# One transposition for both fp16 halves of x, one load for a pair's q and k, and two larger times in the plan of an attention and MLP kernel

## The chip, the cores and the metric

The kernel runs on one core of one Trainium2 chip. The metric is the device time of one execution in microseconds (us), taken as the median of the runs shown. Of one execution there is a profile: for every engine when each instruction ran and what ended its waits. The engines are PE (matrix products; PEld is its weight loads), DVE and ACT (elementwise and reductions, and activation functions), POOL, and SP, which here issues nearly all the DMAs. SPq is SP's queue of DMA issues.

## The reference

```
def phi(x):
    proj = np.einsum('bhsd,df->bhsf', x, w_phi)
    proj = proj - np.max(np.abs(proj), axis=-1, keepdims=True)
    return np.concatenate([np.exp(proj), np.exp(-proj)], axis=-1)
q_p, k_p = (phi(q), phi(k))                          # (8, 8, 576, 256)
kv = np.einsum('bhsf,bhsd->bhfd', k_p, v)
z = np.sum(k_p, axis=2)
num = np.einsum('bhsf,bhfd->bhsd', q_p, kv)
den = np.einsum('bhsf,bhf->bhs', q_p, z)[..., None] + 1e-06
x = num / den, heads side by side: (4608, 512)
h = x @ w_in                                         # w_in (512, 2048)
sp = np.maximum(h, 0.0) + np.log1p(np.exp(-np.abs(h)))
out = (h * erf(sp)) @ w_out                          # w_out (2048, 512)
```

All inputs and the output are float32. The batch is 8, with 8 heads of 64 and 576 tokens.

## The kernel before, in words

Two streams share PE. The attention stream works on pairs of heads, p = 0 to 31, four pairs to a batch, in three groups g of 384 tokens. The MLP stream works on blocks of 256 tokens, in steps n of half a block's hidden width. A large matrix product in float32 is replaced by three in fp16: each operand is split in a high half and a low half, and high by high, high by low and low by high are summed.

For a pair and a group, `k_piece` projects q and k (PE, line L438), takes the row maxima (DVE, tile m, L409) and subtracts them (DVE, tiles uk and uq, L415); ACT writes exp of uk into kp (L359). `t_piece` turns uq, so that features lie on partitions. For the first eight pairs PE does it; from pair 8 on `turn` does: DVE splits the float32 words into 16-bit halves (tile pl, L483), a DMA transposition on SP's queue turns them (plt<-pl, L485, six blocks of 128 columns), and DVE puts them together again (ut<-plt, L486). ACT writes exp of ut into qp (L359). `kv_piece` multiplies kp and v (PE, L352), and `n_piece` multiplies qp and kv (PE, L352), divides by the denominators (DVE, tiles dn and xf) and writes x as two fp16 halves, xth (high) and xtl (low, DVE L561). `x_piece` turns x for the MLP: for each piece of at most 128 tokens one DMA transposition of xth into xh and one of xtl into xl, both on SP's queue (L605), two blocks of 128 columns each.

In the MLP stream `h_chunk` multiplies xh and xl by wih and wil (PE, L342, 128x256), ACT copies the sums out (tile big, L672), softplus and erf follow on DVE and ACT, and `o_chunk` multiplies the gated halves gh and gl by woh and wol (PE, L342, 128x512). The erf gate is one block on ACT: a table load, two activations (L693) and a table load back (L694).

`load_pair` brings a pair's q and k as (two copies of 64 rows beside each other in DRAM, one DMA for k's 64 partitions and one for q's), and v.

The order of all instructions is set by a planner. Every operation states its engine, a cost, and a time `done` after which what it wrote may be used. `Plan.run` plays these through and, whenever an engine is free, takes the ready operation with the lowest priority number; the times at which it starts them give each engine's order of instructions. On the chip each engine then runs its instructions in that order, and waits where an operand isn't there yet. Two numbers matter below. `SLACK`, added to the time from which a PE operation counts as ready, for the operations of MLP steps after n = 2 and the attention pieces laid between them:

```
n.ready = max(n.ready, t + done + (n.slack + 100.0 if n.eng == "PE" else 0.0))
```

And `done=3000` of the transposition in `turn`. Where the plan leaves PE without work for over `HOLE` = 600 ns, it puts in filler products of a constant tile (bank<-hot, L812), two per 216 ns of the hole.

Of the kernel before, what the change touches and what calls it, by code (L numbers as in the profile page):

```python
# [9 lines left out]
F16 = mybir.dt.float16  # L10
# [7 lines left out]
P = 128  # L18
# [5 lines left out]
TB = 256  # L24
# [17 lines left out]
HALVED = 2 * NPAIR  # L42
AHEAD = 8000.0
TURN = 92.0
SLACK = 1200.0
WARM = 10
HOLE = 600.0
PRINT = None
# [23 lines left out]
class Plan:  # L72
# [21 lines left out]
    def buf(self, kind):  # L94
        return Buf(self, kind)
# [161 lines left out]
def favor_attention_moe(ctx: ExitStack, tc: tile.TileContext, qk, vp, wphi, w_in, w_out, out):  # L257
# [10 lines left out]
    def whole(group, n, shape, dt):  # L268
        slots(group, n, shape, dt)
        plan.kind(group, group)  # L270
# [24 lines left out]
    plan.kind("osb", "half", (("osb",), 3))  # L295
    whole("gh", 4, [P, HW], F16)
    whole("gl", 4, [P, HW], F16)
    whole("xh", 8, [P, 2, TB], F16)
    whole("xl", 8, [P, 2, TB], F16)
    slots("ld", 3, [P, 1152], F32)  # L300
    plan.kind("st", "ld", (("st",), 3))
    plan.kind("hl", "ld", (("hl",), 2))
# [12 lines left out]
    whole("kv", 2, [P, 2, 130], F32)  # L315
    whole("dn", 2, [P, 10], F32)
    whole("xf", 2, [P, 256], F32)
    whole("xth", 2, [P, 5, 2 * P], F16)
    whole("xtl", 2, [P, 5, 2 * P], F16)

    op, buf = plan.op, plan.buf
    PE, DVE, ACT, POOL, SP = "PE", "DVE", "ACT", "POOL", "SP"
# [68 lines left out]
    def load_pair(p):  # L391
        t = buf("st")
        for c in [slice(g * 384, (g + 1) * 384) for g in range(3)] if p == 0 else [slice(0, 1152)]:
            for nm, i in (("k", 1), ("q", 0)):
                rows = slice(i * D, (i + 1) * D)
                op(SP, 450 if p == 0 else 600, lambda c=c, i=i, rows=rows: nc.sync.dma_start(t.t[rows, c], qk[p, rows, i, c]),
                   w=[(t, (nm, c.start))], done=2300, land=500 if p == 0 else 1450)
        stg[p] = t, buf("hl") if p >= HALVED else None
        v = buf("v0" if p < NPAIR else "v")
        op(SP, 400, lambda: nc.sync.dma_start(v.t[:, 0:650], vp[p]), w=[v], done=2400, land=1650)  # L400
        vsb[p] = v
# [17 lines left out]
    def project(p, g):  # L419
        kind = "pj" if p >= NPAIR else "p0"  # L420
        src, hl = stg[p]
        both = {nm: buf(kind) for nm in "kq"}
        at = 3 * g * P if p == 0 else 0
        loaded = [(src, ("k", at)), (src, ("q", at))]
        cols = slice(3 * g * P, 3 * (g + 1) * P)
        hv = lambda: hl.t.bitcast(F16).rearrange("p (i t) -> p i t", i=2)
        if hl:
            op(ACT, 430, lambda: nc.scalar.copy(hv()[:, 0, cols], src.t[:, cols]), r=loaded, w=[(hl, (g, 0))], off=-AHEAD)
            op(DVE, 470, lambda: nc.vector.tensor_tensor(hv()[:, 1, cols], src.t[:, cols], hv()[:, 0, cols], op=ALU.subtract),
               r=loaded + [(hl, (g, 0))], w=[(hl, (g, 1))], port=True, off=-AHEAD)  # L430

        def block():
            for t in range(3):
                tok = slice((3 * g + t) * P, (3 * g + t + 1) * P)
                terms = [(hv()[:, 0, tok], w1), (hv()[:, 1, tok], w1), (hv()[:, 0, tok], w2)] if hl else [(src.t[:, tok], wst)]
                for x, w in terms:
                    for nm, rows in (("q", slice(0, D)), ("k", slice(D, P))):
                        nc.tensor.matmul(both[nm].t[:, t * P : (t + 1) * P], x[rows], w.t[rows, :],  # L438
                                         start=w is terms[0][1] and x is terms[0][0], stop=w is terms[-1][1] and x is terms[-1][0])

        if hl:
            op(PE, 520, block, r=[(hl, (g, 0)), (hl, (g, 1)), w1, w2], w=[both["k"], both["q"]], done=780, mode=ROWS)
        else:
            op(PE, 680, block, r=loaded + [wst], w=[both["k"], both["q"]], done=990, mode=ROWS)
        yield 520 if hl else 680
        return front("k", p, both["k"]), front("q", p, both["q"])
# [34 lines left out]
    def turn(u):  # L481
        halves, turned, ut = buf("pl"), buf("plt"), buf("ut")
        op(DVE, 490, lambda: nc.vector.tensor_copy(  # L483
            halves.t, u.t.rearrange("p t f -> p (t f)").bitcast(U16).rearrange("p (n h) -> p h n", h=2)), r=[u], w=[halves], port=True)
        op(SP, 1280, lambda: nc.sync.dma_start_transpose(turned.t, halves.t.rearrange("p h n -> p (h n)")), r=[halves], w=[turned], done=3000)  # L485
        op(DVE, 500, lambda: nc.vector.tensor_copy(  # L486
            ut.t.bitcast(U16).rearrange("p (n h) -> p h n", h=2), turned.t.rearrange("p (h t) k -> p h (t k)", h=2)),
           r=[turned], w=[ut], port=True)
        return ut
# [33 lines left out]
    def n_piece(p, g):  # L523
# [4 lines left out]
        if g == 0:  # L528
            nds[p] = ([buf(kind)], buf("dn"))
            if r == 0:  # L530
                xt[p // 2] = (buf("xth"), buf("xtl"))
        banks, dn = nds[p]
        xth, xtl = xt[p // 2]

        def sums(nb, cnt, h):
            d = lambda: dn.t[:, 6 * h : 6 * h + cnt].unsqueeze(2)
# [5 lines left out]
        def normalise(nb, c0, cnt, d0, key, view):  # L542
            x = buf("xf")
            rows = slice(0, D) if key == "tail" else slice(0, P)
            xv = lambda: x.t[rows, 0 : cnt * D].rearrange("p (t e) -> p t e", t=cnt)
            blk = lambda: nb.t[:, c0 : c0 + 65 * cnt].rearrange("p (t e) -> p t e", e=65)
            d = lambda: dn.t[:, d0 : d0 + cnt].unsqueeze(2)
            if key == "tail":
                for h in range(2):
                    own = slice(h * D, (h + 1) * D)  # L550
                    op(DVE, 140, lambda h=h, own=own: nc.vector.tensor_tensor(
                        xv()[:, h, :], nb.t[own, 0:D], dn.t[own, 0:1].to_broadcast([D, D]), op=ALU.mult),
                       r=[nb, (dn, d0 // 6)], w=[(x, h)])
            else:
                op(DVE, 345, lambda: nc.vector.tensor_tensor(
                    xv(), blk()[:, :, 0:D], d().to_broadcast([P, cnt, D]), op=ALU.mult), r=[nb, (dn, d0 // 6)], w=[x])
            if p < EARLY:
                op(ACT, 310, lambda: nc.scalar.copy(view(xth.t), xv()), r=[x], w=[(xth, (r, key))])
            else:
                op(DVE, 215, lambda: nc.vector.tensor_copy(view(xth.t), xv()), r=[x], w=[(xth, (r, key))], port=True)  # L560
            op(DVE, 345 if cnt == 4 else 205, lambda: nc.vector.tensor_tensor(view(xtl.t), xv(), view(xth.t), op=ALU.subtract),  # L561
               r=[x, (xth, (r, key))], w=[(xtl, (r, key))], port=True)

        def bulk(h):
            return lambda x: x[:, 1:5, r * P + h * D : r * P + (h + 1) * D].rearrange("p t e -> p t e")

        def tail(x):
            return x[0:D, 0, r * P : (r + 1) * P].rearrange("p (t e) -> p t e", t=2)

        for t in range(3):  # L570
            T = 3 * g + t
# [15 lines left out]
                kvs.pop(p)  # L587
                nds.pop(p)

    xh, xl = {}, {}  # L590

    def x_piece(b, half, j):
        n = P if j else 64
        t0 = b * S + ((j - 1) * P if j else 512)
        t = t0
        xth, xtl = xt[2 * b + half]
        while t < t0 + n:
            blk = t // TB
            e = min(t0 + n, (blk + 1) * TB)
            key = blk, half  # L600
            if key not in xh:
                xh[key], xl[key] = buf("xh"), buf("xl")
            for dst, src in ((xh[key], xth), (xl[key], xtl)):
                keys = [(src, (r, k)) for r in range(2) for k in (("tail",) if j == 0 else (0, 1))]
                op(SP, 1280, lambda dst=dst, src=src, t=t, e=e, blk=blk: nc.sync.dma_start_transpose(  # L605
                    dst.t[:, :, t - blk * TB : e - blk * TB], src.t[t - t0 : e - t0, j, :]),
                   r=keys, w=[(dst, t - blk * TB)], done=4300 if b == 0 else 2900)
            t = e
        yield 0

# [43 lines left out]
    def h_chunk(n, c):  # L654
# [5 lines left out]
        for k in range(2):  # L660
            f = half * GF + 2 * c + k
            fs = slice(f * P, (f + 1) * P)
            for cc in range(NCC):
                key = cc, f // 4
                xhb, xlb = xh[blk, cc // 2], xl[blk, cc // 2]
                for w, x, wb in ((wih, xhb, 0), (wih, xlb, 0), (wil, xhb, 1)):
                    mm(109, lambda k=k, cc=cc, fs=fs, w=w, x=x: (ps()[:, k, :], w.t[:, cc, fs], x.t[:, cc % 2, :]),
                       [(w, key), x], [b], cc == 0 and x is xhb and not wb, cc == NCC - 1 and wb == 1)
                    yield 109
        q = c % 2  # L670
        h = hs[n, c // 2]
# [3 lines left out]
            first_evac[n] = o  # L675
        if c == 3 and half:
            for v in range(2):
                xh.pop((blk, v))
                xl.pop((blk, v))

    def softplus(n, v):
        L, h = buf("L"), hs[n, v]
# [146 lines left out]
def _heads_first(x):  # L829
    import numpy as np  # L830

    a = x.reshape(B * NPAIR, 2, S, D)
    return np.concatenate([a[:, 0, 512:], a[:, 1, 512:], a[:, 0, :512], a[:, 1, :512]], axis=1)
# [36 lines left out]
```

## Time and profile before

| | |
|---|---|
| median of 3 runs | 1039.39 us (1038.12 to 1039.76) |
| the profiled execution | 1041.25 us, of which the program's span 1039.5 |
| PE busy | 1012.0 us, 97% of the span, 16732 products |
| DVE, ACT busy | 686.6 us (66%), 710.1 us (68%) |
| mean granted TensorE clock | 0.990 |
| DMA, mean busy share by tenths of the span's fortieths | 8578253437314413233221443334341221000000 |
| transpositions on SP's queue | xh 96, xl 96, plt 72 |
| loads of q and k | 62 of 64x1152, 6 of 64x384 |

A row of the timeline gives start and duration in us, the engine (SPq: a DMA issue), the line, the operation with out<-in, and in brackets how long the engine had sat idle before it and what ended that. Rows of equal neighbours are merged (x6). The answers on waits have total, number of times and the longest, in us. A row of a tile or of a line gives the duration of an instruction in ns as min/median/max. A table of windows gives for each stretch its length and the busy time of each engine in us, then the granted clock of PE and the DMA share.

### The profile page before, as it was taken

The numbers are of one execution on the slowest core, as the hardware profiler recorded it, in microseconds if no ns is written. First come the engines' busy times: TensorE is split into PE (matmuls) and PEld (weight loads), VectorE is DVE, ScalarE is ACT, GpSimd is POOL, SyncE is SP. The second block draws the span as 40 slices with busy tenths as digits, with TensorE's granted clock in tenths as the row PEclk, the third lists the DMA queues.
The fourth block names the chain that finished last, engine by engine and source line by source line (L and its number), as shares of the span: only waits on it lengthen the run. The fifth ranks groups of instructions, "written<-read, shape, count | busy, mean of one in ns | idle before, by whom it ended". The sixth has DMA issues, their size and how long they took to land.

```text
span 1039.5 us, 36968 instructions
## 1 busy us (share of the span) xinstructions
PE 1012.0 (97%) x16732; PEld 790.9 (76%) x16732; DVE 686.6 (66%) x1426; ACT 710.1 (68%) x1126; POOL 0.7 (0%) x6
## 2 busy tenths in 40 slices
PE   9988999998999899999999999999999999999998
PEld 6877876776787777777877777878777777777774
DVE  5989989796658764677644878488756863223332
ACT  6868878776767477766766748676767656566671
POOL 0000000000000000000000000000000000000000
PEclk9999999999999999999999999999999999999999
DMA  8578253437314413233221443334341221000000
GB/s 270 133 166 248 83 187 83 81 63 139 77 41 96 97 43 80 53 77 81 62 51 30 86 88 70 77 64 94 75 85 33 43 60 32 12 22 2 22 12 32
DMA packets 120766, 81.81 MB, mean 79 GB/s; under 512 B 103328, under 2 KB 103840, under 8 KB 120608
## 3 DMA queue, kind: packets, MB, share of 16 engines
q1 hardware_dynamic: 120448, 79.38, 32.0%
q8 instruction: 131, 2.15, 0.9%
q14 instruction: 27, 0.22, 0.1%
q10 hardware_dynamic: 160, 0.07, 0.0%
HBM read 46.37 MB, written 9.44 MB: 54 GB/s over the span
## 4 chain that ended last, share of the span: by engine, by line
PE 72%; DVE 11%; DMA 7%; SPq 5%; ACT 3%; issue 1%; DVEq 0%; ACTq 0%
PE bank L342 58%; PE bank L352 9%; DMA plt<-pl 5%; SPq L605 5%; PE bank L438 4%; DVE m L409 2%; PE bank L812 1%; DVE ut L486 1%; DVE half L380 1%; DVE half L382 1%; DVE uq L415 1%; DMA xh<-xth 1%; DVE wol L386 1%; DVE gl L705 1%; DVE pl L483 1%
## 5 line engine op out<-in xcount | busy, mean ns | idle before, releaser
L342 PE MATMUL bank<-xh,wih 128*64 128x256 f16 x2304 | 321.3, 274 | 2.0 <-DMA xh<-xth 2.0
L342 PE MATMUL bank<-xh,wil 128*64 128x256 f16 x2304 | 321.6, 275 | 0.2 <-DVE wil L386 0.2
L342 PE MATMUL bank<-xl,wih 128*64 128x256 f16 x2304 | 321.8, 275 | 0.0
L342 PEld LDWEIGHTS <-wih 128*64 128x64 f16 x4608 | 257.9, 111 | 31.8 <-DMA xh<-xth 2.1
L342 PE MATMUL bank<-wol,gh 128*64 128x512 f16 x1152 | 221.5, 380 | 0.0
L342 PE MATMUL bank<-woh,gh 128*64 128x512 f16 x1152 | 221.4, 380 | 0.0
L342 PE MATMUL bank<-woh,gl 128*64 128x512 f16 x1152 | 221.3, 379 | 0.0
L342 PEld LDWEIGHTS <-gh 128*64 128x64 f16 x2304 | 128.9, 110 | 81.9 <-issue 0.2
L359 ACT ACTIVATE big<-big 128x1024 f32<-128x1024 f32 x144 | 152.2, 1057 | 41.3 <-DVE big L683 38.7
L672 ACT ACTIVATE big<-bank 128x512 f32<-128x512 f32 x144 | 84.9, 592 | 120.1 <-PE bank L342 119.0
L701 DVE TENSOR_TENSOR big<-big,big 128x1024 f32<-128x1024 f32 x72 | 85.7, 1218 | 83.8 <-ACT big L693 83.8
L342 PEld LDWEIGHTS <-wil 128*64 128x64 f16 x2304 | 132.9, 111 | 3.7 <-DVE wil L386 0.8
L409 DVE TENSOR_REDUCE m<-bank 128x3 f32<-128x384 f32 x192 | 100.0, 549 | 23.2 <-PE bank L438 23.0
L342 PEld LDWEIGHTS <-gl 128*64 128x64 f16 x1152 | 66.2, 110 | 53.7
L359 ACT ACTIVATE qp<-ut 128x384 f32<-128x384 f32 x144 | 69.0, 514 | 55.6 <-DVE ut L486 45.1
L683 DVE TENSOR_SCALAR big<-big 128x1024 f32<-128x1024 f32 x72 | 49.6, 689 | 83.1 <-ACT big L672 82.6
L359 ACT ACTIVATE kp<-uk 128x384 f32<-128x384 f32 x144 | 67.6, 513 | 48.1 <-DVE uk L415 47.8
L705 DVE TENSOR_TENSOR gl<-big,gh 128x1024 f16<-128x1024 f32 x72 | 87.4, 1220 | 15.7 <-ACT gh L704 15.5
L352 PE MATMUL bank<-v,kp 128*64 128x65 f32 (+1 forms) x2016 | 85.0, 231 | 10.1 <-ACT kp L359 9.8
L352 PEld LDWEIGHTS bank<-kv,qp 128*64 128x64 f32 x2304 | 81.6, 139 | 16.8 <-ACT qp L359 9.2
L486 DVE COPY ut<-plt 128x768 uint16<-128x768 uint16 x72 | 43.4, 606 | 75.1 <-DMA plt<-pl 72.1
L352 PE MATMUL bank<-kv,qp 128*64 128x65 f32 x2304 | 85.4, 224 | 7.2 <-ACT qp L359 6.7
(52 smaller groups left out, 1056.1 us busy)
## 6 DMA issues: line engine op xcount, KB each, us to landing
ld<-in_qk_dram SPq DMA_DIRECT2D x62, 288.0 KB, 4.7
out_dram<-half SPq DMA_DIRECT2D x36, 256.0 KB, 2.5
v<-in_vp_dram SPq DMA_DIRECT2D x28, 325.0 KB, 4.2
big<-in_moe_w_in_dram SPq DMA_DIRECT2D x16, 512.0 KB, 9.1
big<-in_moe_w_out_dram SPq DMA_DIRECT2D x16, 512.0 KB, 5.1
xh<-xth SPq DMA_TRANSPOSE x96, 2.5
xl<-xtl SPq DMA_TRANSPOSE x96, 2.4
big<-in_vp_dram SPq DMA_DIRECT2D x4, 325.0 KB, 7.1
```

Of the source, the lines that this page charges most:

```text
L342: nc.tensor.matmul(o[half], a[:, half], b, start=start, stop=stop)
L352: nc.tensor.matmul(o[half], a[:, half], b, start=first and c == 0, stop=last and c == 1)
L359: nc.scalar.activation(out_(), in_(), func, **k)
L380: op(DVE, 600, lambda: nc.vector.scalar_tensor_tensor(f.t.bitcast(I32), word(1), -0x40000000, f.t.bitcast(I32), op0=ALU.bitwise_and, op1=A ...
L409: op(DVE, 470, lambda: nc.vector.tensor_reduce(m.t, ps(), axis=AX.X, op=ALU.max, apply_absolute_value=True), r=[b], w=[m])
L438: nc.tensor.matmul(both[nm].t[:, t * P : (t + 1) * P], x[rows], w.t[rows, :], start=w is terms[0][1] and x is terms[0][0], stop=w is terms ...
L486: op(DVE, 500, lambda: nc.vector.tensor_copy(ut.t.bitcast(U16).rearrange("p (n h) -> p h n", h=2), turned.t.rearrange("p (h t) k -> p h (t ...
L605: op(SP, 1280, lambda dst=dst, src=src, t=t, e=e, blk=blk: nc.sync.dma_start_transpose(dst.t[:, :, t - blk * TB : e - blk * TB], src.t[t - ...
L672: o = op(ACT, 490, lambda: nc.scalar.activation(h.t[:, q * 512 : (q + 1) * 512], b.t, AF.Copy, scale=SG / (SX * SWI)), r=[b], w=[(h, q)])
L683: op(DVE, 602, lambda: nc.vector.tensor_scalar_min(L.t, h.t, CLAMP * SG), r=[h], w=[L], port=True)
L701: op(DVE, 1140, lambda h=h, L=L: nc.vector.tensor_tensor(h.t, h.t, L.t, op=ALU.mult), r=[L, h], w=[h], port=True, off=2000.0 * (v + 1))
L705: op(DVE, 1140, lambda h=h, a=a, b=b: nc.vector.tensor_tensor(b.t, h.t, a.t, op=ALU.subtract), r=[h, a], w=[b], port=True, off=3500.0 * (v ...
```

## The change

Both fp16 halves of x lie in one tile (xt in place of xth and xtl, 4 x 128 columns for each token row), and `x_piece` turns a piece with one transposition of four blocks into one tile (x in place of xh and xl). A pair's q and k lie one after the other in DRAM without the second copy, and `load_pair` brings them with one DMA of 128 partitions. In the plan the turned q block counts as there 4500 ns after its transposition starts (3000 before), and SLACK is 2000 (1200 before). The arithmetic is the same.

```
-SLACK = 1200.0
+SLACK = 2000.0
...
-    whole("xh", 8, [P, 2, TB], F16)
-    whole("xl", 8, [P, 2, TB], F16)
+    whole("x", 8, [P, 4, TB], F16)
...
-    whole("xth", 2, [P, 5, 2 * P], F16)
-    whole("xtl", 2, [P, 5, 2 * P], F16)
+    whole("xt", 2, [P, 5, 4 * P], F16)
...
-            for nm, i in (("k", 1), ("q", 0)):
-                rows = slice(i * D, (i + 1) * D)
-                op(SP, 450 if p == 0 else 600, lambda c=c, i=i, rows=rows: nc.sync.dma_start(t.t[rows, c], qk[p, rows, i, c]),
-                   w=[(t, (nm, c.start))], done=2300, land=500 if p == 0 else 1450)
+            op(SP, 450 if p == 0 else 600, lambda c=c: nc.sync.dma_start(t.t[:, c], qk[p, :, c]),
+               w=[(t, c.start)], done=2300, land=1000 if p == 0 else 2900)
...
-        op(SP, 1280, lambda: nc.sync.dma_start_transpose(turned.t, halves.t.rearrange("p h n -> p (h n)")), r=[halves], w=[turned], done=3000)
+        op(SP, 1280, lambda: nc.sync.dma_start_transpose(turned.t, halves.t.rearrange("p h n -> p (h n)")), r=[halves], w=[turned], done=4500)
...
-            for dst, src in ((xh[key], xth), (xl[key], xtl)):
-                keys = [(src, (r, k)) for r in range(2) for k in (("tail",) if j == 0 else (0, 1))]
-                op(SP, 1280, lambda dst=dst, src=src, t=t, e=e, blk=blk: nc.sync.dma_start_transpose(
-                    dst.t[:, :, t - blk * TB : e - blk * TB], src.t[t - t0 : e - t0, j, :]),
-                   r=keys, w=[(dst, t - blk * TB)], done=4300 if b == 0 else 2900)
+            dst = xs[key]
+            op(SP, 1280, lambda dst=dst, t=t, e=e, blk=blk: nc.sync.dma_start_transpose(
+                dst.t[:, :, t - blk * TB : e - blk * TB], x2.t[t - t0 : e - t0, j, :]),
+               r=keys, w=[(dst, t - blk * TB)], done=4300 if b == 0 else 2900)
```

The rest of the diff follows from it: `n_piece` writes the halves into column ranges of xt, and `h_chunk` reads block `2 * lo + cc % 2` of x (lo is 0 for the high half, 1 for the low one).

The planner's orders move with it. First, SP's queue, where the first two turned q blocks of pair 15 stand (at 333 to 357 us of the profile). The x pieces come in trains, 14 or 10 transpositions long before, eight of each. The end of the seventh train and what stands behind it, before:

```order
L605 DMA_TRANSPOSE xh_98<-xth_150 128x2x128
L605 DMA_TRANSPOSE xl_106<-xtl_152 128x2x128
L605 DMA_TRANSPOSE xh_98<-xth_150 128x2x64
L605 DMA_TRANSPOSE xl_106<-xtl_152 128x2x64
L730 DMA out_dram<-half_89 128x512
L485 DMA_TRANSPOSE plt_141<-pl_139 128x6x128
L485 DMA_TRANSPOSE plt_140<-pl_138 128x6x128
L400 DMA v_118<-in_vp_dram 128x650
L396 DMA ld_115<-in_qk_dram 64x1152 x2
```

The same train after, whole:

```order
L601 DMA_TRANSPOSE x_102<-xt_142 128x4x64
L601 DMA_TRANSPOSE x_104<-xt_142 128x4x64
L601 DMA_TRANSPOSE x_104<-xt_142 128x4x128
L601 DMA_TRANSPOSE x_104<-xt_142 128x4x64
L601 DMA_TRANSPOSE x_98<-xt_142 128x4x64
L601 DMA_TRANSPOSE x_98<-xt_142 128x4x128
L601 DMA_TRANSPOSE x_98<-xt_142 128x4x64
L725 DMA out_dram<-half_89 128x512
L481 DMA_TRANSPOSE plt_133<-pl_131 128x6x128
L481 DMA_TRANSPOSE plt_132<-pl_130 128x6x128
L481 DMA_TRANSPOSE plt_133<-pl_131 128x6x128
L392 DMA ld_106<-in_qk_dram 128x1152
```

The same two turned blocks, plt of pair 15, still stand behind the train, which is 7 long in place of 14; the trains of 10 have become 5. Of all the SP issues that move data, 432 have become 302.

Second, DVE, at the last turned block of pair 27 (the row ut<-plt) and the first block of pair 28 (the rows m and uk on banks 61 and 62 before, 66 and 62 after). Before:

```order
L555 TENSOR_TENSOR xf_148<-bank_65,dn_146 128x256
L516 COPY kv_145<-bank_68 128x260
L560 CAST xth_151<-xf_148 128x4x64
L486 COPY ut_143<-plt_141 128x2x384
L561 TENSOR_TENSOR xtl_153<-xf_148,xth_151 128x4x64
L409 TENSOR_REDUCE m_119<-bank_61 128x3
L409 TENSOR_REDUCE m_120<-bank_62 128x3
L415 TENSOR_TENSOR uk_129<-bank_61,m_119 128x384
L415 TENSOR_TENSOR uq_131<-bank_62,m_120 128x384
```

After:

```order
L551 TENSOR_TENSOR xf_140<-bank_67,dn_138 128x256
L405 TENSOR_REDUCE m_111<-bank_66 128x3
L556 CAST xt_143<-xf_140 128x4x64
L411 TENSOR_TENSOR uk_121<-bank_66,m_111 128x384
L557 TENSOR_TENSOR xt_143<-xf_140,xt_143 128x4x64
L512 COPY kv_137<-bank_68 128x260
L405 TENSOR_REDUCE m_112<-bank_62 128x3
L678 TENSOR_SCALAR big_81<-big_82 128x1024
L411 TENSOR_TENSOR uq_123<-bank_62,m_112 128x384
L482 COPY ut_135<-plt_133 128x2x384
```

The next pair's m, uk and uq have moved from behind the copy that waits for a turned block to ahead of it.

Third, PE, in MLP step 1 (ahead of those that have SLACK), at the second projection of pair 6 (the last row of wphi) and the kv products of that group (v and kp). Before:

```order
L438 MATMUL bank_64<-wphi_70,ld_114 128x128
L438 MATMUL bank_67<-wphi_70,ld_114 128x128
L469 MATMUL bank_66<-ident_69,uq_131 128x128 x3
L352 MATMUL bank_68<-v_117,kp_134 64x65 x12
L342 LDWEIGHTS wih_73
L342 MATMUL bank_65<-xh_101,wih_73 64x256
```

After, the end of a run of filler products and what follows:

```order
L807 LDWEIGHTS hot
L807 MATMUL bank_66<-hot 64x512
L340 LDWEIGHTS wih_73
L340 MATMUL bank_65<-x_101,wih_73 64x256
L350 MATMUL bank_64<-v_109,kp_126 64x65 x4
L465 MATMUL bank_66<-ident_69,uq_123 128x128 x3
```

A run of 32 filler products now stands between the projection and those kv products, and 4 a little ahead of it, while the 6 that stood beside the first MLP products of step 0 (at 68.12 us of the profile) are gone: 130 in all, 100 before. Everywhere else PE has the same products.

More of the change, by code (lines that the diff above doesn't have):

```diff
@@ L423, in project @@
         at = 3 * g * P if p == 0 else 0
-        loaded = [(src, ("k", at)), (src, ("q", at))]
+        loaded = [(src, at)]
         cols = slice(3 * g * P, 3 * (g + 1) * P)
@@ L530, in n_piece @@
             if r == 0:
-                xt[p // 2] = (buf("xth"), buf("xtl"))
+                xt[p // 2] = buf("xt")
         banks, dn = nds[p]
-        xth, xtl = xt[p // 2]
+        x2 = xt[p // 2]
         def sums(nb, cnt, h):
@@ L557, in normalise, with tail @@
             if p < EARLY:
-                op(ACT, 310, lambda: nc.scalar.copy(view(xth.t), xv()), r=[x], w=[(xth, (r, key))])
+                op(ACT, 310, lambda: nc.scalar.copy(view(0), xv()), r=[x], w=[(x2, (r, key, 0))])
             else:
-                op(DVE, 215, lambda: nc.vector.tensor_copy(view(xth.t), xv()), r=[x], w=[(xth, (r, key))], port=True)
-            op(DVE, 345 if cnt == 4 else 205, lambda: nc.vector.tensor_tensor(view(xtl.t), xv(), view(xth.t), op=ALU.subtract),
-               r=[x, (xth, (r, key))], w=[(xtl, (r, key))], port=True)
+                op(DVE, 215, lambda: nc.vector.tensor_copy(view(0), xv()), r=[x], w=[(x2, (r, key, 0))], port=True)
+            op(DVE, 345 if cnt == 4 else 205, lambda: nc.vector.tensor_tensor(view(1), xv(), view(0), op=ALU.subtract),
+               r=[x, (x2, (r, key, 0))], w=[(x2, (r, key, 1))], port=True)
         def bulk(h):
-            return lambda x: x[:, 1:5, r * P + h * D : r * P + (h + 1) * D].rearrange("p t e -> p t e")
-        def tail(x):
-            return x[0:D, 0, r * P : (r + 1) * P].rearrange("p (t e) -> p t e", t=2)
+            return lambda i: x2.t[:, 1:5, (2 * i + r) * P + h * D : (2 * i + r) * P + (h + 1) * D]
+        def tail(i):
+            return x2.t[0:D, 0, (2 * i + r) * P : (2 * i + r + 1) * P].rearrange("p (t e) -> p t e", t=2)
         for t in range(3):
@@ L588, in n_piece @@
                 nds.pop(p)
-    xh, xl = {}, {}
+    xs = {}
     def x_piece(b, half, j):
@@ L595, in x_piece @@
         t = t0
-        xth, xtl = xt[2 * b + half]
+        x2 = xt[2 * b + half]
+        keys = [(x2, (r, k, i)) for r in range(2) for k in (("tail",) if j == 0 else (0, 1)) for i in range(2)]
         while t < t0 + n:
@@ L600, in x_piece @@
             key = blk, half
-            if key not in xh:
-                xh[key], xl[key] = buf("xh"), buf("xl")
-            for dst, src in ((xh[key], xth), (xl[key], xtl)):
-                keys = [(src, (r, k)) for r in range(2) for k in (("tail",) if j == 0 else (0, 1))]
-                op(SP, 1280, lambda dst=dst, src=src, t=t, e=e, blk=blk: nc.sync.dma_start_transpose(
-                    dst.t[:, :, t - blk * TB : e - blk * TB], src.t[t - t0 : e - t0, j, :]),
-                   r=keys, w=[(dst, t - blk * TB)], done=4300 if b == 0 else 2900)
+            if key not in xs:
+                xs[key] = buf("x")
+            dst = xs[key]
+            op(SP, 1280, lambda dst=dst, t=t, e=e, blk=blk: nc.sync.dma_start_transpose(
+                dst.t[:, :, t - blk * TB : e - blk * TB], x2.t[t - t0 : e - t0, j, :]),
+               r=keys, w=[(dst, t - blk * TB)], done=4300 if b == 0 else 2900)
             t = e
@@ L664, in h_chunk @@
                 key = cc, f // 4
[L665 to L668, printed above, removed]
+                x = xs[blk, cc // 2]
+                for i, (w, lo) in enumerate(((wih, 0), (wih, 1), (wil, 0))):
+                    mm(109, lambda k=k, cc=cc, fs=fs, w=w, x=x, lo=lo: (ps()[:, k, :], w.t[:, cc, fs], x.t[:, 2 * lo + cc % 2, :]),
+                       [(w, key), x], [b], cc == 0 and i == 0, cc == NCC - 1 and i == 2)
                     yield 109
@@ L677, in h_chunk @@
             for v in range(2):
-                xh.pop((blk, v))
-                xl.pop((blk, v))
+                xs.pop((blk, v))
     def softplus(n, v):
@@ L843 @@
         lay[n] = np.ascontiguousarray(inputs[n]).view(np.int64)
-    qk = np.stack([_heads_first(inputs[nm]).transpose(0, 2, 1) for nm in ("q", "k")], axis=2)
-    lay["qk"] = np.concatenate([qk, qk], axis=1)
+    lay["qk"] = np.concatenate([_heads_first(inputs[nm]).transpose(0, 2, 1) for nm in ("q", "k")], axis=1)
     v = _heads_first(inputs["v"]).reshape(B * NPAIR, 9, P, D).transpose(0, 2, 1, 3)
```

## The prediction

> **What bounds the kernel now.** PE is busy for 1012.0 of the 1039.5 us. What can be won without taking products away is therefore PE's idle time, and the time in which it runs at a lower clock. I read first the clock of the core, then PE's waits, then each wait at its place, then back from it through ACT and DVE to SP's queue.
>
> The core's row gives the mean granted clock, the rows below it PE's waits (total, times, longest):
>
> ```profile
> core 0: 1039.5 us, clock 0.990
> ...
> PE bank L352 <- ACT kp L359: 9.8, 7, 2.6
> PE bank L352 <- ACT qp L359: 6.7, 3, 2.9
> PE bank L342 <- DMA xh<-xth: 2.0, 1, 2.0
> ...
> PE bank L438 <- DVE xf L555: 1.1, 3, 0.5
> PE bank L438 <- DVE uk L415: 0.6, 1, 0.6
> PE bank L342 <- DVE wil L386: 0.2, 1, 0.2
> ```
>
> The first five rows are 20.2 us of idle. A clock of 0.990 over the span is another 10.3 us. Both are few large events. The timeline of PE has the instructions behind the long waits:
>
> ```profile
> 67.87 0.41 PE L342 MATMUL bank<-xh,wih 128*64 128x256 f16 x4 [1.96 <-DMA xh<-xth]
> 99.49 0.74 PE L352 MATMUL bank<-v,kp 128*64 128x65 f32 x8 [2.60 <-ACT kp L359]
> 199.73 0.34 PE L352 MATMUL bank<-kv,qp 128*64 128x65 f32 x4 [2.12 <-ACT qp L359]
> 240.21 0.34 PE L352 MATMUL bank<-kv,qp 128*64 128x65 f32 x4 [1.70 <-ACT qp L359]
> 251.31 0.34 PE L352 MATMUL bank<-v,kp 128*64 128x65 f32 x4 [1.59 <-ACT kp L359]
> 261.09 0.34 PE L352 MATMUL bank<-v,kp 128*64 128x65 f32 x4 [1.09 <-ACT kp L359]
> 357.99 0.34 PE L352 MATMUL bank<-kv,qp 128*64 128x65 f32 x4 [2.90 <-ACT qp L359]
> 625.00 0.50 PE L352 MATMUL bank<-v,kp 128*64 128x130 f32 x6 [1.45 <-ACT kp L359]
> 736.17 0.44 PE L352 MATMUL bank<-v,kp 128*64 128x130 f32 x4 [1.98 <-ACT kp L359]
> ```
>
> The table of windows shows the clock around them (the third number from the end is PEclk):
>
> ```profile
> 68.20:71.60 3.40, 3.40 (x30) 2.37 (x28) 3.16 (x7) 0.61 (x2) 0.00 (x0) 0.50 0.23 40
> ...
> 98.90:105.70 6.80, 6.18 (x62) 5.09 (x64) 6.80 (x13) 6.61 (x17) 0.00 (x0) 0.50 0.57 181
> ...
> 201.30:204.70 3.40, 3.40 (x52) 2.68 (x48) 2.39 (x8) 2.82 (x6) 0.00 (x0) 0.51 0.93 196
> 239.00:243.00 4.00, 2.72 (x72) 2.51 (x74) 3.46 (x8) 3.02 (x6) 0.00 (x0) 1.00 1.01 233
> ...
> 358.30:361.70 3.40, 3.32 (x50) 2.69 (x50) 3.40 (x7) 3.30 (x7) 0.00 (x0) 0.51 0.91 237
> ...
> 737.20:740.60 3.40, 3.40 (x49) 2.61 (x46) 1.67 (x4) 1.51 (x2) 0.00 (x0) 0.50 0.54 140
> ```
>
> After each wait of 1.96 us or more PE runs at half clock for 3.4 us (6.8 once), 20.4 us in all, which is the 10.2 us that the mean clock lacks. After the wait of 1.70 us (window 239 to 243) the clock stays at 1.00. So a long wait costs its idle time and 1.7 us more, and the one at 99.49 us costs 2.6 and 3.4. The Trainium skill ("TensorE: Matmul & The Clock Gate", Part 1) has the clock fall to half only after at least one idle window of about 3.4 us; by that none of these waits, all under 3 us, would cost a slow stretch. The trace disagrees with it here: 1.96 us did.
>
> Where the wait at 357.99 comes from: SP issues x transpositions without a break, and two turned q blocks stand behind them; DVE sits at the copy of the turned block, ACT at its exp.
>
> ```profile
> 332.82 1.17 SPq L605 DMA_TRANSPOSE xl<-xtl  x1
> ...
> 350.87 1.23 SPq L605 DMA_TRANSPOSE xl<-xtl  x1
> ...
> 352.77 2.48 SPq L485 DMA_TRANSPOSE plt<-pl  x1
> ...
> 356.78 0.60 DVE L486 COPY ut<-plt 128x768 uint16<-128x768 uint16 x1 [5.33 <-DMA plt<-pl]
> ...
> 357.41 0.94 ACT L359 ACTIVATE qp<-ut 128x384 f32<-128x384 f32 x2 [5.69 <-DVE ut L486]
> ```
>
> The waits for kp have the same root once removed, since DVE takes its instructions in order: at 736.17 the maxima and uk of the next pair stand behind a copy that waits for a turned block. Over the kernel DVE waits so 35 times:
>
> ```profile
> 733.19 0.61 DVE L486 COPY ut<-plt 128x768 uint16<-128x768 uint16 x1 [1.13 <-DMA plt<-pl]
> ...
> 734.02 1.01 DVE L409 TENSOR_REDUCE m<-bank 128x3 f32<-128x384 f32 x2
> 734.95 0.55 DVE L415 TENSOR_TENSOR uk<-bank,m 128x384 f32<-128x384 f32 x1
> ...
> DVE ut L486 <- DMA plt<-pl: 72.1, 35, 5.3
> ```
>
> **The change part by part.** The rows for SP's queue (ns min/median/max of an issue, then us to landing, first of x, then of plt):
>
> ```profile
> L605 SPq DMA_TRANSPOSE xh<-xth x96: 1159/1238/2738, 37.5 to 871.2; - x96
> ...
> DMA to landing us min/median/max: 2.3/2.4/7.9
> ...
> L485 SPq DMA_TRANSPOSE plt<-pl x72: 1210/1232/2475, 160.2 to 847.4; - x72
> ...
> DMA to landing us min/median/max: 2.7/2.8/6.0
> ...
> L396 SPq DMA_DIRECT2D ld<-in_qk_dram x68: 465/578/1776, 0.7 to 774.2; - x68
> ...
> L400 SPq DMA_DIRECT2D v<-in_vp_dram x28: 327/352/1375, 12.7 to 801.4; - x28
> ```
>
> *The x transposition.* A transposition of two blocks occupies the queue for 1.238 us, one of six for 1.232, so the issue does not grow with the blocks, and four blocks lie between: 1.24. The 96 that go take 96 x 1.24 = 119 us off SP's queue; a train of 14 is about 8.7 us shorter, one of 10 about 6.2. Landing lies between 2.4 and 2.8 us, I take 2.6; the low half used to land 1.24 + 2.4 = 3.6 us after the first issue, so a piece is there 1 us earlier. If against the rows the queue paid by blocks, an issue would take 2.48 and the trains would be as long as now; that end is a rival below. The queue itself is on the path only through what waits for it.
>
> *The load.* One DMA of 128 partitions has its price between the row of 64 rows (0.58) and that of v, which has 128 partitions (0.35); by its form it is nearest to v. Some 31 times two issues of 0.58 become one of 0.35 to 0.58: 18 to 25 us less on SP. It carries the same bytes to SBUF, so I leave its landing (median of one half 4.6) as it is. PE itself waits for no load by name; nothing is counted for this part alone.
>
> *The first x pieces* (67.87 us). The piece that ended this wait stands behind others of its train; with half the issues it lands some four issues, 5 us, earlier, against a wait of 1.96. The wait and its slow stretch go: -1.96 - 1.7 = -3.7 (ends: 0 and -3.7). Late next are the products' own weights, split by DVE, which held PE for 0.2 us.
>
> *The fillers.* The rows of the wait at 99.49 and of a run of fillers:
>
> ```profile
> 94.46 1.28 ACT L693 ACT_TABLE_LOAD   x1
> ...
> 99.07 0.37 ACT L359 ACTIVATE kp<-bank,mb 128x128 f32<-128x128 f32 x1
> ...
> 13.30 1.46 PE L812 MATMUL bank<-hot 128*64 128x512 f16 x12
> ```
>
> ACT is in the erf block from 94.46 to 99.07 with kp behind it. That block stays. The new order puts 32 fillers where PE had this wait. At 1.46/12 = 0.12 us each, the 30 additional ones are 3.6 us of PE work. They replace 2.60 us of idle and keep the clock up, which is worth 3.4: 3.6 - 2.6 - 3.4 = -2.4. If the block is not under way when they run, they are lost entirely and the wait remains: +3.6 is the other end.
>
> *The turned blocks* (everything after 110 us). At 357.99 the train ahead of the two blocks shrinks by 8.7 us, three times the wait of 2.90: -2.9 - 1.7 = -4.6. At 199.73 the train is 14 as well, and the wait goes: -2.1 - 1.7 = -3.8. At 240.21 the train is one of 10, 6.2 us against a wait of 1.70: -1.7. What is left is in waits behind DVE's copy: kp at 251.31, 261.09, 625.00 and 736.17 with 1.59 + 1.09 + 1.45 + 1.98 and one slow stretch of 1.7, and the 1.1 and 0.6 us of L438, 9.5 in all. Here it is the plan's 4500 ns, and not the queue, that acts: DVE's order has more work between putting the halves into pl and fetching ut, and at 736.17 the next pair's m and uk now stand ahead of the copy. A landing can take up to 6.0 us, more than 4500 ns, so I count half: -5.0 (ends: 0 and -9.5). Together -15.1.
>
> *SLACK.* It puts 0.8 us more between a producer and the PE product that uses it, in MLP steps after n = 2, at no cost on PE as long as other products are there to take the place, and the order shows no fillers after 110 us, so they are. Its benefit is in the terms above. Without that cover the cost would be a filler of 0.12 us for each 0.108 us of hole.
>
> *New waits.* Every operation has moved, and waits that were covered can come out. The old order had nine waits over 1 us; two new ones of 1.7 us, the size that keeps the clock, are my estimate: +3.4 (ends: 0, and 6.8 with four).
>
> The sum: -3.7 - 2.4 - 15.1 + 3.4 = -17.8 us. The profiled execution took 1041.25 us (span 1039.5 and 1.75 around it) and comes to 1023.4; the median of the runs, 1039.39, is 1.9 us lower and comes to 1021.6. I say 1022. If all 20.2 us of idle and 10.2 of slow clock went, and the fillers stayed, it would be 1039.4 - 30.4 + 3.6 = 1012.6: the lower bound.
>
> **The rivals.**
>
> *The waits move instead of going.* The order of three engines is fixed ahead, landings scatter from 2.7 to 6.0 us, and whatever stands behind the latest landing waits. For it: the old plan foresaw none of its waits either. Against it: a queue with 119 us less to issue has fewer late turns. Then only the first two terms hold: 1039.4 - 6.1 = 1033.3.
>
> *Transpositions of four blocks hold the queue twice as long.* Against it stand the two rows with equal issue times; for it, that some issues in a train take 2.5 us. The trains are then as long as now, the terms for 67.87, 199.73, 240.21 and 357.99 fail, and -2.4 - 5.0 + 3.4 = -4.0 is left: 1035.4.
>
> *The slow stretches stay.* They might come from PE's load over a longer time and not from these waits. The sum loses 1.7 at each of 67.87, 199.73 and 357.99, 3.4 at 99.49 and half of 1.7 at 736.17, 9.4 us: 1031.0. Against it: five slow stretches, and each follows one of the five waits of 1.96 us or more. The rule of the Trainium skill quoted above is on this side, in that it ties no slow stretch to waits as short as these.
>
> *Slower: projections wait for their bank.* Projections and numerators share three banks, and a numerator's bank is free only when DVE has divided (xf). DVE now fetches ut later in its order; if what divides comes later with it, each projection waits for xf, as three did (1.1 us in all, 0.5 the longest). At 0.5 us for two of the three projections of each of the 24 pairs from 8 on, that is +24: 1021.6 + 24 = 1046. It decides from 17.8/24 = 0.74 us for each pair on. Against it: those three waits are all that the profile has.
>
> **How the numbers follow.** The forecast gets 0.66, with a range of its own from 1013 to 1031 (all the waits gone; half the term of the turned blocks failing and four new waits). The waits that move get 0.15, the queue that pays by blocks 0.06, the slow stretches that stay 0.05, the slower case 0.08. The range for 8 in 10 goes from 1012 to 1035, which takes in the second and third rivals and leaves out the slower one and the edges of the others. About 0.2%, 2 us, is what a measurement of this kernel can tell from no change. Faster by more: nearly all of the forecast's 0.66, 0.12 of the first rival, most of the other two: 0.85. Slower: the slower case and a little of the first rival, 0.09. Within: 0.06.
>
> **What would show it.** SP's rows: 96 transpositions of x at 1.24 us each, trains of 7 in 9 to 10 us. DVE's wait for plt<-pl well under 72 us. No PE wait for x at the first MLP products, a run of fillers where the wait of 2.60 us was. PE's waits for kp and qp from 16.5 to under 8 us, and a mean clock of 0.995 or more. The prediction is wrong if an issue of four blocks takes 2 us or more, if PE waits for kp and qp as long as before at other places, or if the fillers run and the wait of the erf block stands behind them as well.

## The result and the profile after

| | before | after |
|---|---|---|
| median of the runs | 1038.76 us (4 runs, 1033.26 to 1039.76) | 1010.26 us (4 runs, 1010.11 to 1010.70) |
| ratio, 95% interval | | 0.9737 (0.9702 to 0.9772) |
| the profiled execution | 1041.25 us, span 1039.5 | 1010.18 us, span 1008.4 |

The kernel is 2.6% faster, 28.5 us between the medians and 31.1 between the profiled spans. The forecast was 1022 with a range from 1012 to 1035: the direction was right, the gain was forecast at 17.8 and is 28.5, and the time lies below the range.

The clock's row, the page's first row and, from the page, the chain that ended last, of after:

```profile
core 0: 1008.4 us, clock 1.000
...
PE 1000.3 (99%) x16762; PEld 784.5 (78%) x16762; DVE 685.9 (68%) x1426; ACT 708.8 (70%) x1126; POOL 0.7 (0%) x6
...
PE 96%; DVE 3%; DMA 0%; ACT 0%; issue 0%
```

The same two rows of the page of before, for the comparison that follows:

```profile
PE 1012.0 (97%) x16732; PEld 790.9 (76%) x16732; DVE 686.6 (66%) x1426; ACT 710.1 (68%) x1126; POOL 0.7 (0%) x6
...
PE 72%; DVE 11%; DMA 7%; SPq 5%; ACT 3%; issue 1%; DVEq 0%; ACTq 0%
```

The span without PE's busy time was 1039.5 - 1012.0 = 27.5 us and is 8.1: 19.4 us of idle are gone. PE's busy time fell by 11.7 us although it has 30 products more. The chain of before went through DVE, DMA and SP's queue for a quarter of the span; after it is PE's own.

All the waits of PE that the trace of after names, then what DVE still waits for turned blocks (total, times, longest):

```profile
PE bank L434 <- DVE uq L411: 1.6, 1, 1.6
PE bank L807 <- DVE hot L813: 1.5, 1, 1.5
PE bank L350 <- ACT kp L357: 0.8, 1, 0.8
PE bank L340 <- ACT half L357: 0.6, 1, 0.6
...
DVE ut L482 <- DMA plt<-pl: 22.2, 9, 6.3
```

Not one of the nine waits shown in the prediction is left. The second row is the start of the kernel, and the third is an early wait of 0.75 us that before has too, at 59.50. DVE's wait fell from 72.1 us in 35 places to 22.2 in 9.

SP's queue, after: the issues of x, of plt and of the loads (ns min/median/max), the landing of x, and the seventh train:

```profile
L601 SPq DMA_TRANSPOSE x<-xt x96: 1170/1248/2622, 37.0 to 831.5; - x96
...
DMA to landing us min/median/max: 2.3/2.4/5.0
...
L481 SPq DMA_TRANSPOSE plt<-pl x72: 1209/1217/2073, 153.0 to 810.3; - x72
...
L392 SPq DMA_DIRECT2D ld<-in_qk_dram x34: 327/428/536, 0.7 to 738.6; - x34
...
311.88 10.86 SPq L601 DMA_TRANSPOSE x<-xt  x7
322.85 0.51 SPq L725 DMA_DIRECT2D out_dram<-half  x1
323.46 2.59 SPq L481 DMA_TRANSPOSE plt<-pl  x2
```

Four blocks occupy the queue for 1.248 us and land after 2.4. The train is 7 long and takes 10.9 us, some issues in it 2.6 us.

### The profile page after: what moved, and what is told of

Same layout as the page of the kernel before. It is cut to its first block, busy times and chain, and to the rows that moved or that the text cites. A ratio compares the mean times of both kernels' runs of the same rounds, so it can differ in the third digit from the quotient of the medians.

```text
span 1008.4 us, 36824 instructions
## 1 busy us (share of the span) xinstructions
PE 1000.3 (99%) x16762; PEld 784.5 (78%) x16762; DVE 685.9 (68%) x1426; ACT 708.8 (70%) x1126; POOL 0.7 (0%) x6
## 4 chain that ended last, share of the span: by engine, by line
PE 96%; DVE 3%; DMA 0%; ACT 0%; issue 0%
PE bank L340 73%; PE bank L350 14%; PE bank L434 6%; PE bank L807 2%; PE bank L465 1%; DVE m L405 1%; DVE gl L700 0%; DMA plt<-pl 0%; DVE uq L411 0%; DVE big L696 0%; DVE uk L411 0%; DVE ld L425 0%; DVE xt L557 0%; DVE pl L479 0%; DVE ut L482 0%
## 5 line engine op out<-in xcount | busy, mean ns | idle before, releaser
L340 PE MATMUL bank<-x,wih 128*64 128x256 f16 x4608 | 395.6, 273 | 0.6 <-ACT half L357 0.6
L340 PE MATMUL bank<-x,wil 128*64 128x256 f16 x2304 | 318.6, 273 | 0.0
L340 PEld LDWEIGHTS <-wih 128*64 128x64 f16 x4608 | 254.7, 110 | 29.6 <-issue 1.4
L340 PEld LDWEIGHTS <-wil 128*64 128x64 f16 x2304 | 130.8, 110 | 2.4
L357 ACT ACTIVATE qp<-ut 128x384 f32<-128x384 f32 x144 | 67.4, 513 | 22.2 <-DVE ut L482 18.7
L350 PE MATMUL bank<-v,kp 128*64 128x65 f32 (+1 forms) x2016 | 82.1, 228 | 0.8 <-ACT kp L357 0.8
L350 PE MATMUL bank<-kv,qp 128*64 128x65 f32 x2304 | 82.7, 222 | 0.0
L350 PEld LDWEIGHTS bank<-v,kp 128*64 128x64 f32 x2016 | 76.4, 137 | 7.7 <-ACT kp L357 1.6
L699 ACT CAST gh<-big 128x1024 f16<-128x1024 f32 x72 | 74.0, 1039 | 9.7 <-DVE big L696 9.6
```

The costliest lines, as they stand in the source:

```text
L340: nc.tensor.matmul(o[half], a[:, half], b, start=start, stop=stop)
L350: nc.tensor.matmul(o[half], a[:, half], b, start=first and c == 0, stop=last and c == 1)
L357: nc.scalar.activation(out_(), in_(), func, **k)
L699: op(ACT, 940, lambda h=h, a=a: nc.scalar.copy(a.t, h.t), r=[h], w=[a], off=2500.0 * (v + 1))
```

## The experiments

Two theories were set against each other. Q: SP's queue, paid by the issue, made the turned blocks late, and everything else followed. P: the order of DVE and PE, which the planner made with too short a time for a turned block and too little slack, stood in the wrong places, whatever the queue did. Each ratio is against before on the same chip; "order" means that of all instructions of each engine.

**e1, the order of before, one transposition for both halves.** The planner goes through the same operations as before with the same costs; the first operation of a piece issues nothing, the second issues the transposition of four blocks.

```
-                op(SP, 1280, lambda dst=dst, src=src, t=t, e=e, blk=blk: nc.sync.dma_start_transpose(
-                    dst.t[:, :, t - blk * TB : e - blk * TB], src.t[t - t0 : e - t0, j, :]),
+                def issue(both=xh[key], src=xth, t=t, e=e, blk=blk, i=i):
+                    if i:
+                        nc.sync.dma_start_transpose(both.t[:, :, t - blk * TB : e - blk * TB], src.t[t - t0 : e - t0, j, :])
+                op(SP, 1280, issue,
```

> The order of every engine is that of before, instruction for instruction, except that SP issues one transposition of four blocks where it issued two of two (96 in place of 192). Theory Q (the time on SP's queue makes the turned blocks late, and that is the whole cause): nearly all the waits go without a new order, 1039 less some 25, about 1014 us, clock 0.998. Theory P (the order matters: DVE stands at the copy of a turned block too early, whatever the queue does): only the waits that end a train go (67.87, 199.73, 240.21, 357.99 us: 8.7 us idle and 5.1 of slow clock), the one of the erf block at 99.49 and those for kp stay: about 1025 us, DVE's wait for plt still over 50 us.

1013.58 us, ratio 0.9765 (0.974 to 0.979). PE's waits and DVE's:

```profile
PE bank L356 <- ACT kp L363: 3.3, 2, 2.6
PE bank L820 <- DVE hot L826: 1.5, 1, 1.5
PE bank L356 <- issue: 1.0, 1, 1.0
PE bank L442 <- DVE uk L419: 0.6, 1, 0.6
PE bank L442 <- DVE xf L559: 0.5, 1, 0.5
DVE ut L490 <- DMA plt<-pl: 31.8, 17, 4.4
```

With not one instruction moved on PE, DVE and ACT, most of the gain is there. The waits for qp are gone (6.7 us before). Those for kp are 3.3 us in place of 9.8, and the 2.6 of them is the erf block's wait, which this order keeps. That is theory Q. Theory P's 1025 is well outside the interval.

**e2, the order of after, two transpositions.** The reverse of e1: the planner sees one operation, and it issues two of two blocks each.

```
+            def issue(dst=dst, t=t, e=e, blk=blk):
+                for i in range(2):
+                    nc.sync.dma_start_transpose(dst.t[:, 2 * i : 2 * i + 2, ...], x2.t[..., j, 2 * P * i : 2 * P * (i + 1)])
```

> The order of every engine is that of after, except that SP issues two transpositions of two blocks where it issued one of four (192 in place of 96). Theory Q: the trains are 14 and 10 long again, the planner did not allow for them, and the waits come back, 1035 us or more, clock 0.99. Theory P: DVE's order gives 4500 ns and PE's 2000, some of the lateness is absorbed: about 1020 us. By both SP is busy some 133 us longer with x than after.

1067.88 us, ratio 1.0286 (1.0255 to 1.0316): not only is the gain gone, it is slower than before by 29.5 us. Two rows of the waits:

```profile
PE bank L350 <- ACT kp L357: 29.2, 6, 7.7
...
DVE ut L482 <- DMA plt<-pl: 109.7, 19, 14.1
```

Both theories were too low. The order of before was made for 192 issues, the order of after for 96. That it therefore asks for its turned blocks earlier than the longer queue can bring them is a reading and not measured by itself; what the trace shows is that DVE's longest wait for one is 14.1 us (5.3 in before), and the plan's 4500 ns are small against that.

**e5, the order and data of after, and behind each transposition of x a spare one of 16 tokens.**

```
                 nc.sync.dma_start_transpose(dst.t[:, :, t - blk * TB : e - blk * TB], x2.t[t - t0 : e - t0, j, :])
+                nc.sync.dma_start_transpose(spare[len(turns) % 6], x2.t[t - t0 : t - t0 + 16, j, 0:P])
```

> The order and the data of after; behind each of the 96 transpositions of x SP issues one more, of a single block of 16 tokens into a spare tile that nobody reads. Theory Q in the form 'each issue costs the queue 1.24 us, whatever it carries': 96 x 1.24 = 119 us more on SP and the same lateness as with two issues of two blocks, 1060 to 1070 us. If it was the bytes, or two halves landing one after the other, that made e2 slow: the spare block carries 1/32 of the data, no product waits for it, and the time stays at 1010 to 1015.

1069.45 us, ratio 1.0299 (1.0265 to 1.0332), as e2. The issue times of x and of the spare block:

```profile
L604 SPq DMA_TRANSPOSE x<-xt x96: 1170/1252/2362, 36.6 to 896.8; - x96
...
L605 SPq DMA_TRANSPOSE spare<-xt x96: 1111/1223/2622, 37.9 to 898.1; - x96
```

DVE waits 114.0 us for turned blocks, 14.8 the longest, against 109.7 and 14.1 in e2. The spare block has 1/32 of the data of a piece of 128 tokens, and 1/16 where the piece has 64, as half of the pieces do; nobody waits for it, and it does the same harm as a whole half of x. What costs is the issue, 1.22 us of the queue with so little to carry; bytes and the landing of the second half are not the cause.

**e6, the order of before, one transposition and one load.** As e1, and in `load_pair` the first of the two operations issues nothing, the second issues the load of 128 partitions.

```
+                fetch = (lambda c=c: nc.sync.dma_start(t.t[:, c], qk[p, :, c])) if i else (lambda: None)
```

> As e1 (every engine in the order of before, one transposition of x in place of two), and also one load of q and k in place of two. Theory Q: the load takes another 31 x 0.6 to 0.8 = 20 us off SP, some of the 2.4 us of kp waits and the late copies go: 1010 to 1013. If the load is nothing (its landing as before, SP no longer short): 1013.6, as e1.

1010.76 us, ratio 0.9728 (0.9701 to 0.9755): the same as after. So shorter work on SP alone gives the whole gain, in the old order.

**e9, the order of before, one load alone**, with two transpositions of x as before; the edit is the line of e6.

> The order of before on every engine, two transpositions of x as before; alone the load of q and k is one issue in place of two. Theory Q (SP's queue, by issue): 31 x 0.7 us off SP, not in the trains but in the gaps between the turned blocks; a small part of the gain, 1033 to 1037. If the load were what the sum of e1 and e6 says (1013.6 to 1010.8) also in a crowded queue: 1035. If nothing: 1038.

1034.01 us, ratio 0.9973 (0.9951 to 0.9994): a small gain, 2.8 us by the ratio (0.6 to 5.1).

**e10, the order of after, two loads.**

```
+            def fetch(c=c):
+                for i in (1, 0):
+                    nc.sync.dma_start(t.t[i * D : (i + 1) * D, c], qk[p, i * D : (i + 1) * D, c])
```

> The order of after on every engine; the load of q and k in two issues of 64 partitions. Theory Q: 20 us more on SP, spread in ones of 0.7 us, in a queue that has room: 1010 to 1014.

1012.61 us, ratio 0.9766 (0.9748 to 0.9784). Its median lies 2 to 3 us above after's, which ran on another chip, and the intervals overlap: small, and not settled.

**e4, before with the x transposition of both halves alone, in a new order** (SLACK 1200, `done=3000`, two loads).

> Before with one change, the x transposition of both halves, and the planner's order that follows from it; SLACK 1200, 3000 ns for a turned block, two loads for a pair. Theory Q: most of the gain, about 1015 us. Theory P: the waits behind DVE's copy stay, about 1026 us.

1015.94 us, ratio 0.9788 (0.9767 to 0.9808). Not to be told apart from e1; the planner's own new order for it is no better than the old one.

**e11, before with 4500 alone, in a new order.**

```
-        op(SP, 1280, lambda: nc.sync.dma_start_transpose(turned.t, ...), r=[halves], w=[turned], done=3000)
+        op(SP, 1280, lambda: nc.sync.dma_start_transpose(turned.t, ...), r=[halves], w=[turned], done=4500)
```

> Before with done=4500 for the turned block, and the planner's new order; two transpositions of x, two loads, SLACK 1200. Theory Q: SP has as much to issue as before, the plan only knows more of it; the landing terms go (about 5 us), trains stay: 1030 to 1036. Theory P: 1020 to 1025.

1020.91 us, ratio 0.9843 (0.982 to 0.9866). Theory P's number came out here, with SP's 192 transpositions untouched:

```profile
PE bank L352 <- ACT kp L359: 3.8, 3, 2.6
PE bank L342 <- DMA xh<-xth: 2.0, 1, 2.0
PE bank L812 <- DVE hot L818: 1.4, 1, 1.4
PE bank L352 <- ACT qp L359: 1.4, 1, 1.4
...
DVE ut L486 <- DMA plt<-pl: 39.5, 19, 4.8
```

The wait for the first x pieces stays, as it must, since nothing of x changed; the waits for qp and kp are down to 5.2 us in all, from 16.5 in before (3.3 in e1). The profiled execution, of 1017.83 us, is the fastest of its four. The late blocks can be made early, or DVE can be told to do something else meanwhile; either takes most of the same waits.

**e7, after with `done=3000`**, the reverse edit of e11, in a new order.

> After with done=3000 for the turned block, all else as after; the planner makes its order anew. Theory Q: SP's queue has room, the landing takes 2.8 us, and the plan's number no longer matters: 1010 to 1012. Theory P: the waits behind DVE's copy come back, 5 us or more: 1015 or more.

1017.88 us, ratio 0.9804 (0.9773 to 0.9836), against 0.9702 to 0.9772 for after. Theory Q's 1010 to 1012 is excluded. One long wait, at a projection, makes most of it:

```profile
184.28 0.40 PE L434 MATMUL bank<-w,ld 64*128 64x128 f16 x8 [4.19 <-DVE uq L411]
```

DVE waits 63.2 us for turned blocks in this kernel, nearly as long as before: with 3000 the planner puts the copies too early again, also with 96 transpositions.

**e8, after with SLACK 1200; e12, before with SLACK 2000**, each in a new order.

> After with SLACK=1200, all else as after; the planner makes its order anew. Theory Q: 1010 to 1012. Theory P: PE waits again by up to 0.8 us at some of the products that follow DVE or ACT, 3 to 6 us in all: 1013 to 1016.

> Before with SLACK=2000 and the planner's new order, all else as before. Theory Q: 0.8 us of distance against waits of 1.1 to 2.9 us; some fall below 1.9 us and keep the clock: 1030 to 1037. Theory P: 1025 to 1030.

1011.92 us, ratio 0.974 (0.9713 to 0.9768), and 1037.42 us, ratio 0.9996 (0.9975 to 1.0017): SLACK does nothing that can be measured, with the crowded queue or with the short one.

**e3, after without the fillers of MLP step 1**, 36 of them, all else in the same order.

```
-            if e == "PE" and free[e] and t - free[e] > HOLE:
+            if e == "PE" and free[e] and t - free[e] > HOLE and t < 70000.0:
```

> The changed kernel without the 36 filler products that the planner put in MLP step 1, all else in the same order. If the fillers are what keeps the erf block's wait from slowing the clock (the prediction's term): the wait of 2.6 us or more comes back with a slow stretch of 3.4 or 6.8 us, and 3.6 us of fillers go: +2.4 us, 1012.7. If PE would not have waited there any more (the fillers are lost time): -3.6 to -4 us, 1006.5.

1011.2 us, ratio 0.9739 (0.972 to 0.9757), not to be told apart from after by the runs. The traces show why: the row of the 32 fillers in after, and what stands there in e3, with its clock in the 3.9 us behind the wait:

```profile
90.79 3.64 PE L807 MATMUL bank<-hot 128*64 128x512 f16 x32
```

```profile
94.33 0.41 PE L340 MATMUL bank<-x,wih 128*64 128x256 f16 x4 [3.48 <-ACT wih L357]
...
94.50:98.40 3.90, 3.90 (x43) 2.87 (x41) 3.90 (x8) 3.90 (x12) 0.00 (x0) 0.56 0.71 231
```

PE would wait there for 3.48 us, about as long as the fillers run, and the slow clock behind it costs some 1.7 more: the spans are 1009.6 and 1008.4.

## Why the prediction was wrong, point by point

**What bounds the kernel, and the root of the waits: right.** PE's waits and the slow clock were nearly all there was to win (what was missing stands under the bound of 1012.6), and they led back to SP's queue. e1 and e6 show it with PE's order unchanged.

**The x transposition: right.** An issue of four blocks takes 1.248 us (1.24 taken), the landing 2.4 (2.6 taken). The rival in which the queue pays by blocks needed 2.48 us for an issue and is out; e5 says the same. Only the train of 7 was longer than said, 10.9 us and not 9 to 10, since some issues in it take up to 2.6.

**The first x pieces: right**, -3.7 forecast; the wait and its slow stretch are gone.

**The fillers: right in sum.** After has no wait and full clock there, as forecast; e3 shows that the fillers run in time that PE would otherwise have lost, so they are neither cost nor much of a gain.

**The turned blocks: this step failed, in size.** It gave -15.1. The waits after 110 us were 14.9 us and their slow stretches 5.1, all of it went: 20.0. The sentence that was wrong is "it is the plan's 4500 ns, and not the queue, that acts", with half of 9.5 us counted for it. In e1, with `done=3000` and DVE's order as before, the kp waits went too. The queue was behind these as well: a late block delays DVE, and DVE everything after it. And 4500 alone takes 16.7 us off the median (e11), not the 5 of the term. With the short queue it counts only where the planner makes a new order: e7, without it, is some 7 us slower than after, while e6 in the old order does as well as after without it. Two remedies for one cause, each worth most of it, had been written as two terms, one certain and one half certain.

**New waits: too dear.** +3.4 forecast; after has 1.6 + 0.6 at new places, and neither slowed the clock.

**The bound of 1012.6: this step failed too.** It added up the idle that the waits' rows name and the slow clock, and took that for all there was. PE's busy time fell by 11.7 us: 10.2 are the slow stretches (20.4 us at half clock), and 30 more fillers at 0.114 (3.64/32 from the row above) take 3.4 back, so 4.9 us of busy time went that no row had called idle. e1 shows where such time lies. There PE runs the same 16732 products in the same order as before, and yet its busy time is 11.6 us less:

```profile
PE 1000.4 (99%) x16732; PEld 783.6 (77%) x16732; DVE 686.3 (68%) x1426; ACT 709.0 (70%) x1126; POOL 0.7 (0%) x6
```

Laid beside each other product by product, the two traces differ by 6.5 us in the slow stretches of before and by 5.2 outside them. Of these 5.2, 4.8 lie at only 23 products: 18 stand behind a gap, and at the other five hardly any overlap with the product ahead was left. For products overlap: at 240.21 us of before the first product behind the wait adds its whole 0.271 us to PE's busy time, and the same product in e1, in a stream without a gap, adds 0.055. So a wait cost about 0.2 us more than its row and its slow stretch say, and this part is counted as busy. Gaps under 0.15 us, which get no row, were another 1.1 us in before and 0.1 in after. The bound, taken from the profiled 1041.25 us, was 1014.5; less 4.9 and 1.0, and with 2.2 of new waits, it is 1010.8, against 1010.18 in the profiled execution of after.

Together: between the two profiled executions the forecast is -17.8 and the result -31.1. Of the 13.3 us between them 4.9 (turned blocks), 1.2 (new waits), 4.9 (busy time behind waits) and 1.0 (short gaps) are 12.0; the rest is not assigned.

**The load:** nothing was counted. Its issue took 0.428 us, between the 0.35 and 0.58 of the prediction. e9 shows 0.6 to 5.1 us in the crowded queue. In the short one it is not settled (e10).

**SLACK:** its benefit was put into the terms above; e8 and e12 show none.

**The rivals.** That the waits move is out for this change, but e7 is a case of it: its order has a wait of 4.19 us that neither before nor after has. The slower rival, projections waiting for a bank, did not come: no wait for xf is left. That the slow stretches would stay without the waits is out: the mean clock is 1.000.

## What to carry to other kernels

Where an in-order queue is shared, count issues and not only bytes: a merged transposition cost one issue here, and everything behind it on that queue, and on the engines that wait in order for it, came earlier. When two edits cure the same lateness, test each alone before adding them up, since either may take nearly all of it. The order that was made for the short queue was worse than the old one when the queue was not short (1067.88 against 1038.39 us): a planner's costs have to be those that the chip shows. And a wait costs more than its row: add what the first product behind it takes.

## What the runs showed of the hardware

An issue of a DMA transposition occupied SP's queue for 1.22 us with 16 tokens of one block and 1.25 us with four blocks of 128; in a train of 7 the mean was 10.86/7 = 1.55.

How long PE must wait before its clock halves is not sharp. The prediction took 1.96 us as enough. In e9 a wait of 2.72 us, and in e11 one of 2.05, left the clock at full speed; the clock is again the third number from the end:

```profile
350.56 0.69 PE L352 MATMUL bank<-kv,qp 128*64 128x65 f32 x6 [2.72 <-ACT qp L359]
...
350.60:354.00 3.40, 3.32 (x80) 2.88 (x82) 3.40 (x8) 3.37 (x7) 0.00 (x0) 1.00 0.67 257
```

```profile
66.99 0.41 PE L342 MATMUL bank<-xh,wih 128*64 128x256 f16 x4 [2.05 <-DMA xh<-xth]
...
67.00:70.40 3.40, 3.40 (x58) 3.09 (x60) 3.38 (x7) 1.28 (x3) 0.00 (x0) 1.00 0.21 46
```

The Trainium skill ("TensorE: Matmul & The Clock Gate", Part 1) describes a window of fixed length that runs freely and watches how busy PE is; with such a window the same wait can halve the clock or not, by where it falls. The traces agree with that, and with its length of about 3.4 us in the slow stretches of 3.4 and 6.8. They do not agree with a whole window of idle as the condition, since waits of 1.96 to 2.9 us were enough in before.

What counts in these traces is where the idle time falls. The clock changes only on a fixed grid of 3.413 us: the five slow stretches of before begin at 68.22, 98.94, 201.34, 358.35 and 737.23 us, and the distances, 30.72, 102.40, 157.01 and 378.88 us, are 9, 30, 46 and 111 times 3.413. In the cells of this grid just before them PE was busy for 1.45, 1.36, 1.44, 0.49 and 1.43 us. The wait of 1.70 us, which kept the clock, lies in a cell with 2.02. The cell ahead of 201.34 and the cell of that wait (PE's busy time is the second number):

```profile
197.93:201.34 3.41, 1.44 (x36) 1.25 (x37) 2.82 (x6) 2.19 (x4) 0.00 (x0) 1.00 0.89 210
...
238.89:242.30 3.41, 2.02 (x52) 1.88 (x52) 3.30 (x7) 2.32 (x6) 0.00 (x0) 1.00 1.03 241
```

The longer wait of e9 is divided between two cells, with 1.48 and 2.55 us of busy time, and the cell with most of e11's wait has 1.56. Over the 14 traces of this case, every cell at full clock in which PE was busy for less than 43% of the time (36 of them) was followed by half clock; of 49 cells with 43 to 70% four were, and of those above none. For those four PE's busy share is not the whole rule, and what else counts is open.
